# q transposed by the vector engine in 32x32 blocks, scores in 32x32 tensor-engine tiles: a fused attention and maxout kernel on one Trainium2 core

## The chip, the cores and the metric

The kernel runs on one core of a Trainium2 chip. The metric is the device time of one execution in microseconds (us). A profile shows a span from the first to the last instruction, which for this kernel is about 1.8 us shorter than the time. The granted clock is the TensorE clock that the profile records, as a share of full speed. A few executions fall into a much slower state (one of the kernel before at 287.87 us); these are left out of every comparison.

The engines: PE is TensorE (matmuls; PEld are its weight loads), DVE is VectorE, ACT is ScalarE, POOL is GpSimd (here it issues the input DMAs), SP is SyncE (the output DMAs). To evacuate a tile is to copy it from PSUM, where matmuls write, to SBUF. ffn is the part with w1, w2, w3 and w_out.

## The reference, cut to what matters

```python
# q, k, v: (8, 8, 576, 64); phi: (8, 8, 576, 32); float32
a    = softmax(phi, axis=2)                        # over the 576 tokens
k_m  = einsum('bhsm,bhsd->bhmd', a, k)             # 32 memory slots per head
v_m  = einsum('bhsm,bhsd->bhmd', a, v)
attn = softmax(q @ k_m^T / 8, axis=-1)             # 576 x 32 per head
x    = (attn @ v_m).transpose(0, 2, 1, 3).reshape(4608, 512)
h    = maximum(maximum(x @ w1, x @ w2), x @ w3)    # 512 -> 768
out  = h @ w_out                                   # 768 -> 512
```

The kernel folds v_m into w1, w2 and w3 for each batch, and works with w1 - w3 and w2 - w3, so that the maxout is a relu, a maximum, and w3 @ w_out added at the end.

One remark on correctness. With these inputs the scores are so small that every softmax over the 32 slots is nearly flat: computing the reference on a CPU with q set to zero changes the result by 8e-7 of its norm. So a comparison of results says next to nothing about whether the tokens of q are in the right order.

## The kernel before

A partition holds nine consecutive tokens of a head (`c` = 0..8), a pair of heads fills 128 partitions, and each of the 8 batches has four pairs (`j`). PE transposes q in 128x128 pieces into PSUM and DVE copies them to SBUF; columns then come in chunks, all tokens with the same `c` together.

```python
def att_q(b, jj):                      # jj = 0, 1: two pairs each; jj = 2: the ninth chunk
    ...
    pt = one_pool.tile([P, 2, NCP - 1, P], BF16, name="pt", tag="one")
    for i in range(2):
        for c in range(NCP - 1):
            nc.tensor.transpose(pt[:, i, c, :], qq[:, 2 * jj + i, 2 * c : 2 * c + 2, :], ident)
    nc.vector.tensor_copy(out=qT[:, 2 * jj : 2 * jj + 2, x : x + NCP - 1, :], in_=pt)
    ...

def att_score(b, g):                   # 64x32 tiles: 8 matmuls a step, two steps a batch
    ...
    nc.tensor.matmul(sc[M * j : M * (j + 1), par, 0 : nch * HP],
                     lhsT=km[par][r, g, j, :],
                     rhs=qT[r, j, c0 : c0 + nch, HP * g : HP * (g + 1)],
                     start=True, stop=True, tile_position=(HP * par, M * j))
    ...                                # exp on ACT, one call for each par
```

The order of all instructions is written by hand as a list of steps: Q transposes q, S the scores, M and R the softmax sums and reciprocals, X the multiply that gives attn, D the folds, F the twelve pieces of the first ffn layer, T the output tiles, E, B, N, K the phi exponentials, the k/v sums, their normalising and transposing. A plus sign means the next batch, two or three the ones after that, a minus sign the batch before. The steady loop is:

```python
run(b, "F0 F6 F1 F8 F4 F7 F2 F5 F10 F3 F9 T2- S0+ D1+ S1+ T3- Q0++ M0+ R0+")
run(b, "M1+ F11 Q1++ T0 R1+ T4- Q2++ E+++ D0+ X0+ B++ D3+ X1+ N++ D2+ T1 K++")
```

Output tiles are evacuated by DVE except one (`EVAC = {"D": "avaa", "T": "vvvav"}`, a for ACT, v for DVE), collected in pairs, and written by two DMAs a pair.

The softmax here doesn't subtract the row's maximum and nothing guards it: scores larger than these inputs give would overflow.

## Time and profile before

| | before |
|---|---|
| time, median of the fast runs | 186.08 us (185.88, 186.08, 186.31; a fourth run was slow) |
| span of the profiled run | 184.2 us |
| PE, DVE, ACT busy | 170.7, 110.1, 100.3 us |
| granted TensorE clock | 0.981 |
| last matmul to end of span | 6.3 us (177.9 to 184.2) |

The page gives each engine's busy time, then the span in 40 slices with a digit for the busy tenths, then the chain that ended last, followed back from the last instruction through whatever released each step. A microsecond saved off this chain is worth nothing until the chain moves. The lines themselves stand in the prediction.

### The profile page before, as it was taken

To read this page: it belongs to the slowest core of one execution; us is meant where nothing else is said; L and a number is where in the kernel's file an instruction comes from. 1 tells how busy PE (TensorE), PEld (TensorE's weight loads), DVE (VectorE), ACT (ScalarE), POOL (GpSimd) and SP (SyncE) were. 2 spreads that over 40 slices of the span, in tenths; PEclk is the share of its full clock that TensorE was granted. 3 is DMA by queue.
4 is the path that set the end of the run, shared out by engine and by line. 5 is a ranking of instruction groups with operands and counts; after the bars stand their busy time and mean duration, and the time that the engine had idled before them with its cause. 6 is when DMAs were issued, how large, how long until landed. Compare 5 with 4: busy or idle time off the path is not lost.

```text
span 184.2 us, 4510 instructions
## 1 busy us (share of the span) xinstructions
PE 170.7 (93%) x1940; PEld 97.8 (53%) x1940; DVE 110.1 (60%) x187; ACT 100.3 (54%) x158; POOL 28.3 (15%) x43
## 2 busy tenths in 40 slices
PE   7997997899999799999999999999999999999960
PEld 2454633554556557464756574657565744565420
DVE  5407338597396677757676677576766773564410
ACT  4100836846696776486637864866376646842010
POOL 7841121043212330005100400000000000000000
PEclk9999699999999999999999999999999999999996
DMA  5999999999999999998999699423021404240545
GB/s 155 162 208 208 209 210 273 208 276 206 272 255 222 308 228 253 255 216 261 287 253 188 112 197 249 120 62 92 25 57 62 114 4 116 57 114 4 136 94 168
DMA packets 21893, 31.75 MB, mean 172 GB/s; under 512 B 1265, under 2 KB 16369, under 8 KB 21873
## 3 DMA queue, kind: packets, MB, share of 16 engines
q0 software_dynamic: 16080, 21.43, 61.5%
q1 hardware_dynamic: 5792, 10.03, 19.6%
q8 instruction: 15, 0.25, 0.5%
q14 instruction: 6, 0.04, 0.1%
HBM read 39.32 MB, written 9.44 MB: 265 GB/s over the span
## 4 chain that ended last, share of the span: by engine, by line
PE 61%; DMA 23%; ACT 4%; POOL 4%; issue 3%; DVE 2%; POOLq 0%
PE po L412 22%; PE acc L385 22%; DMA w_sb<-in_moe_w_dram 12%; DMA qq<-in_q_dram 11%; PE po L421 6%; PE wps L360 3%; PE pt L262 2%; ACT wp L152 2%; POOL kvo L99 2%; PE sm L316 1%; PE po L430 1%; PE sc L292 1%; DVE w_sb L187 1%; POOL w_sb L113 1%; ACT r L335 1%
## 5 line engine op out<-in xcount | busy, mean ns | idle before, releaser
L385 PE MATMUL acc<-attn,wp 128*128 128x288 bf16 x384 | 52.5, 286 | 0.7 <-DVE wp L154 0.7
L412 PE MATMUL po<-wo_sb,hT 128*128 128x512 bf16 x216 | 52.6, 380 | 0.0
L397 DVE TENSOR_TENSOR hT<-acc,h 128x576 bf16<-128x576 f32 x48 | 35.5, 755 | 17.2 <-PE acc L385 16.0
L385 PEld LDWEIGHTS <-wp 128*128 128x128 bf16 x384 | 36.5, 98 | 13.2 <-DVE wp L154 1.0
L395 ACT ACTIVATE h<-acc 128x576 bf16<-128x576 f32 x48 | 29.7, 651 | 19.2 <-PE acc L385 19.2
L412 PEld LDWEIGHTS <-hT 128*128 128x128 bf16 x216 | 19.8, 98 | 23.9 <-issue 3.8
L154 DVE COPY ost<-po 128x512 f32<-128x512 f32 x24 | 16.6, 691 | 19.2 <-PE po L421 19.2
L152 ACT CAST wp<-wps 128x1024 bf16<-128x1024 f32 x24 | 23.4, 1014 | 7.9 <-PE wps L360 7.9
L302 ACT ACTIVATE e<-sc 128x320 bf16<-128x320 f32 (+1 forms) x32 | 10.7, 415 | 26.6 <-PE sc L292 26.6
L421 PE MATMUL po<-wp,attn 128*128 128x512 bf16 x64 | 19.0, 379 | 0.0
L265 DVE COPY qT<-pt 128x1024 bf16<-128x1024 bf16 x16 | 10.9, 686 | 6.8 <-PE pt L262 6.7
L143 PE MATMUL po<-warm 128*128 128x512 bf16 x44 | 12.6, 450 | 1.2 <-DVE warm L131 1.2
L152 ACT COPY ost<-po 128x512 f32<-128x512 f32 x8 | 4.7, 586 | 15.3 <-PE po L421 15.3
L107 POOL DMA_DIRECT2D qq<-in_q_dram x8 | 6.0, 744 | 43.1 <-PE pt L271 33.0
L329 ACT ACTIVATE ln<-sm 128x576 f32<-128x576 f32 x16 | 10.3, 645 | 2.2 <-PE sm L316 1.8
L340 DVE TENSOR_TENSOR attn<-e,r 128x576 bf16<-128x576 bf16 x16 | 11.4, 745 | 0.0
L360 PE MATMUL wps<-w_sb,vk 64*32 64x512 bf16 x96 | 9.3, 382 | 2.1 <-DVE w_sb L187 1.3
L335 ACT ACTIVATE r<-ln 128x576 f32<-128x576 f32 x16 | 10.9, 683 | 0.5
L204 ACT ACTIVATE e<-ph 128x1152 bf16<-128x1152 f32 (+1 forms) x9 | 9.5, 1051 | 2.2 <-DMA ph<-in_phi_dram 2.2
L262 PE MATMUL pt<-ident,qq 128*128 128x128 bf16 x128 | 9.6, 219 | 1.1 <-DMA qq<-in_q_dram 1.1
L421 PEld LDWEIGHTS <-attn 128*128 128x128 bf16 x64 | 6.3, 98 | 7.4
L262 PEld LDWEIGHTS <-qq 128*128 128x128 bf16 x128 | 8.2, 98 | 3.2 <-DMA qq<-in_q_dram 1.6
(51 smaller groups left out, 155.7 us busy)
## 6 DMA issues: line engine op xcount, KB each, us to landing
out_dram<-ost SPq DMA_DIRECT2D x32, 256.0 KB, 3.5
qq<-in_q_dram POOLq DMA_DIRECT2D x8, 576.0 KB, 17.6
ph<-in_phi_dram POOLq DMA_DIRECT2D x7, 576.0 KB, 18.6
kvo<-in_k_dram POOLq DMA_DIRECT2D x7, 576.0 KB, 17.5
kvo<-in_v_dram POOLq DMA_DIRECT2D x7, 576.0 KB, 19.5
w_sb<-in_moe_w_dram POOLq DMA_DIRECT2D x3, 768.0 KB, 19.0
out_dram<-ot SPq DMA_DIRECT2D x8, 128.0 KB, 2.4
wo_sb<-in_moe_w_out_dram POOLq DMA_DIRECT2D x1, 768.0 KB, 16.1
```

Source lines behind the costliest of these rows:

```text
L143: nc.tensor.matmul(po[:, 0:BANK], lhsT=warm[:, 0:P], rhs=warm, start=True, stop=True)
L152: nc.scalar.copy(out=out_, in_=in_)
L154: nc.vector.tensor_copy(out=out_, in_=in_)
L262: nc.tensor.transpose(pt[:, i, c, :], qq[:, 2 * jj + i, 2 * c : 2 * c + 2, :], ident)
L335: nc.scalar.activation(out=r, in_=ln, func=AF.Exp, scale=-1.0)
L340: nc.vector.tensor_tensor(out=attns[b // 2][:, g, (b % 2) * S : (b % 2 + 1) * S], in0=s["e2"][:, g, 0:S], in1=s["r", g], op=ALU.mult,)
L360: nc.tensor.matmul(ps[M * j : M * (j + 1), a, :], lhsT=s["vm"][a][r, a, j, :], rhs=w12[r, j, n * BANK : (n + 1) * BANK] if n < 3 else w3o[ ...
L385: nc.tensor.matmul(acc[:, h, 0:SH], lhsT=wps[b][:, g, w * DF + ft * P : w * DF + (ft + 1) * P], rhs=attn[:, g, c0 : c0 + SH], start=(g == ...
L395: nc.scalar.activation(out=h1, in_=a, func=AF.Relu)
L397: nc.vector.tensor_tensor(out=hT[:, ft, (b % 2) * S : (b % 2 + 1) * S].rearrange("p (h n) -> p h n", h=2), in0=a, in1=s["h1", ft], op=ALU.max,
L412: nc.tensor.matmul(po, lhsT=hT[:, fc, c0 : c0 + P], rhs=wo_sb[:, fc, :], start=(fc == 0), stop=False,)
L421: nc.tensor.matmul(po, lhsT=attn[:, g, c0 : c0 + P], rhs=wp3s[b][:, g, :], start=False, stop=(g == NG - 1),)
```

## The change

The intent: free PE of 160 transposes of q, by letting DVE transpose 32x32 blocks directly from SBUF to SBUF. The write of that transpose puts the tokens into their true order, so 128 columns are 128 consecutive output rows and each output tile is one plain DMA. As only 32 of the 64 head dimensions then share a block row, the scores become 32 matmuls a batch in sixteen 32x32 tiles, accumulated over two halves. Work is shared out anew between ACT and DVE, and the instruction order is new. The core of the diff:

```diff
-    EVAC = {"D": "avaa", "T": "vvvav"}
+    EVAC = {"D": "aass", "T": "aaava"}      # s: half on ACT, half on DVE
 ...
-    def att_q(b, jj):
+    def att_q(b, n):
 ...
+            s["qT"] = work.tile([P, NP, 2, SH], BF16, name="qT")
+        nc.vector.transpose(
+            out=s["qT"][:, :, n].rearrange("p j (r c) -> p j c r", c=NC),
+            in_=loaded[b]["q"].rearrange("p j c d -> p (j c) d")[:, :, R * n : R * (n + 1)],
+        )
 ...
+        for h in range(2):
+            for j in range(NP):
+                for a in range(NG):
+                    for t in range(2):
+                        r = slice(R * (2 * a + t), R * (2 * a + t + 1))
+                        nc.tensor.matmul(
+                            sc[a][M * j : M * (j + 1), t, 0:SH],
+                            lhsT=kvt[r, 1 + h, M * j : M * (j + 1)],
+                            rhs=qT[r, j, h, :],
+                            start=(h == 0),
+                            stop=(h == 1),
+                            tile_position=(R * (2 * a + t), M * j),
+                        )
 ...
+        ot = opool.tile([P, DM], FP32, name="ot")
+        evacuate("T", t, ot, po)
+        r0 = (b // 2) * 2 * S + c0
+        nc.sync.dma_start(out=out[r0 : r0 + P, :], in_=ot)
 ...
-        run(b, "F0 F6 F1 F8 F4 F7 F2 F5 F10 F3 F9 T2- S0+ D1+ S1+ T3- Q0++ M0+ R0+")
-        run(b, "M1+ F11 Q1++ T0 R1+ T4- Q2++ E+++ D0+ X0+ B++ D3+ X1+ N++ D2+ T1 K++")
+        run(b, "S+ B++ N++ D0+ T4- F0 F10 F1 F8 F11 F4 F2 F5 F6 E+++ F7 K++ F9 M0+ T3-")
+        run(b, "M1+ Q0++ F3 R0+ R1+ T2- D2+ D1+ D3+ X1+ Q1++ T1 T0 X0+")
```

`(r c) -> c r` means that the 32 elements of one block row are written nine elements apart: 2-byte elements at a step of 18 bytes.

More of the change, by code (lines that the diff above doesn't have):

```diff
@@ L37 @@
     NC = S // HP
-    NCP = (NC + 1) // 2
+    R = 32
     DM = H * D
@@ L41 @@
     FT = DF // P
-    EVEN = NCP * HP
     SH = S // 2
@@ L49 @@
     quad = ctx.enter_context(tc.tile_pool(name="quad", bufs=4))
+    opool = ctx.enter_context(tc.tile_pool(name="opool", bufs=6))
     acc_pool = ctx.enter_context(
@@ L145, in warm_up @@
             )
-    EVAC = {"D": "avaa", "T": "vvvav"}
+    EVAC = {"D": "aass", "T": "aaava"}
     def evacuate(kind, n, out_, in_):
-        if EVAC[kind][n] == "a":
+        e = EVAC[kind][n]
+        if e == "s":
+            nc.scalar.copy(out=out_[:, 0], in_=in_[:, 0])
+            nc.vector.tensor_copy(out=out_[:, 1], in_=in_[:, 1])
+        elif e == "a":
             nc.scalar.copy(out=out_, in_=in_)
@@ L228, in att_kv_norm @@
         nc.vector.reciprocal(out=rden, in_=kvp[:, :, 2 * D])
-        kvn = work.tile([P, NG, 2 * D], BF16, name="kvn")
+        kvn = work.tile([P, 3, P], BF16, name="kvn")
+        nc.vector.tensor_tensor(
+            out=kvn[:, 0].rearrange("p (a d) -> p a d", a=NG),
+            in0=kvp[:, :, D : 2 * D],
+            in1=rden.unsqueeze(2).to_broadcast([P, NG, D]),
+            op=ALU.mult,
+        )
         for g in range(NG):
+            kn = kvn[:, 1:3, HP * g : HP * (g + 1)]
             nc.vector.tensor_scalar_mul(
-                out=kvn[:, g], in0=kvp[:, g, 0 : 2 * D], scalar1=rden[:, g : g + 1]
+                out=kn.rearrange("p h (t d) -> p h t d", t=2),
+                in0=kvp[:, g, 0:D]
+                .rearrange("p (h d) -> p h d", h=2)
+                .unsqueeze(2)
+                .to_broadcast([P, 2, 2, R]),
+                scalar1=rden[:, g : g + 1],
             )
@@ L238, in att_kv_t @@
         s = st[b]
-        kvt = one_pool.tile([P, NG, NP, M], BF16, name="kvt", tag="one")
-        for g in range(NG):
-            nc.tensor.transpose(kvt[:, g], s["kvn"][:, g], ident)
-        kv = work.tile([P, NG, NP, M], BF16, name="kv")
-        nc.vector.tensor_copy(out=kv, in_=kvt)
-        vk = work.tile([P, NG, NP, M], BF16, name="vk")
-        for u in range(2):
-            nc.vector.tensor_copy(
-                out=vk[HP * u : HP * (u + 1)], in_=kvt[HP * (1 - u) : HP * (2 - u)]
-            )
@@ L249, in att_kv_t @@
-        s.update(km=(kv, vk), vm=(vk, kv))
-    def att_q(b, jj):
+        ps = one_pool.tile([P, 3, P], BF16, name="kvtp", tag="one")
+        for n in range(3):
+            nc.tensor.transpose(ps[:, n], s["kvn"][:, n], ident)
+        kvt = work.tile([P, 3, P], BF16, name="kvt")
+        nc.vector.tensor_copy(out=kvt, in_=ps)
+        s["kvt"] = kvt
+    def att_q(b, n):
         s = st.setdefault(b, {})
-        qq = loaded[b]["q"]
         if "qT" not in s:
-            s["qT"] = work.tile([P, NP, NCP, P], BF16, name="qT")
-        qT = s["qT"]
-        x = b % 2
-        if jj < NP // 2:
-            pt = one_pool.tile([P, 2, NCP - 1, P], BF16, name="pt", tag="one")
-            for i in range(2):
-                for c in range(NCP - 1):
-                    nc.tensor.transpose(
-                        pt[:, i, c, :], qq[:, 2 * jj + i, 2 * c : 2 * c + 2, :], ident
-                    )
-            nc.vector.tensor_copy(
-                out=qT[:, 2 * jj : 2 * jj + 2, x : x + NCP - 1, :], in_=pt
-            )
-        else:
-            pt = one_pool.tile([P, NP, P], BF16, name="pt", tag="one")
-            for j in range(NP):
-                nc.tensor.transpose(pt[0:HP, j, :], qq[:, j, NC - 1, :], ident)
-            nc.vector.tensor_copy(
-                out=qT[0:HP, :, 0 if x else NCP - 1, :], in_=pt[0:HP]
-            )
@@ L276 @@
-    attns = {}
-    def att_score(b, g):
-        s = st[b]
-        km, qT = s["km"], s["qT"]
-        x = b % 2
-        if "e2" not in s:
-            s["e2"] = work.tile([P, NG, S + HP], BF16, name="e2")
-            if x == 0:
-                attns[b // 2] = work.tile([P, NG, 2 * S], BF16, name="attn")
-        sc = acc_pool.tile([P, 2, BANK], FP32, name="sc", tag="acc")
-        for par in range(2):
-            nch = NCP - par
-            c0 = x * par
-            r = slice(HP * par, HP * (par + 1))
-            for j in range(NP):
-                nc.tensor.matmul(
-                    sc[M * j : M * (j + 1), par, 0 : nch * HP],
-                    lhsT=km[par][r, g, j, :],
-                    rhs=qT[r, j, c0 : c0 + nch, HP * g : HP * (g + 1)],
-                    start=True,
-                    stop=True,
-                    tile_position=(HP * par, M * j),
-                )
-        for par in range(2):
-            nch = NCP - par
+            s["qT"] = work.tile([P, NP, 2, SH], BF16, name="qT")
@@ new lines, in att_q, with att_score @@
+        nc.vector.transpose(
+            out=s["qT"][:, :, n].rearrange("p j (r c) -> p j c r", c=NC),
+            in_=loaded[b]["q"].rearrange("p j c d -> p (j c) d")[:, :, R * n : R * (n + 1)],
+        )
+    attns = {}
+    def att_score(b):
+        s = st[b]
+        kvt, qT = s["kvt"], s["qT"]
+        e2 = s["e2"] = work.tile([P, NG, S], BF16, name="e2")
+        if b % 2 == 0:
+            attns[b // 2] = work.tile([P, NG, 2 * S], BF16, name="attn")
+        sc = [
+            acc_pool.tile([P, 2, BANK], FP32, name="sc", tag="acc") for _ in range(NG)
+        ]
+        for h in range(2):
+            for j in range(NP):
+                for a in range(NG):
[8 more added lines that the diff above has]
+                            tile_position=(R * (2 * a + t), M * j),
+                        )
+        for a in range(NG):
@@ L302, in att_score @@
             nc.scalar.activation(
-                out=s["e2"][:, g].rearrange("p (c u n) -> p c u n", u=2, n=HP)[
-                    :, 0:nch, par, :
-                ],
-                in_=sc[:, par, 0 : nch * HP].rearrange("p (c n) -> p c n", n=HP),
+                out=e2[:, a].rearrange("p (t n) -> p t n", t=2),
+                in_=sc[a][:, :, 0:SH],
                 func=AF.Exp,
@@ L361, in fold @@
                     ps[M * j : M * (j + 1), a, :],
-                    lhsT=s["vm"][a][r, a, j, :],
+                    lhsT=s["kvt"][r, 0, M * j : M * (j + 1)],
                     rhs=w12[r, j, n * BANK : (n + 1) * BANK] if n < 3 else w3o[r, j, :],
@@ L437, in ffn2 @@
                     )
-        if t < 4:
-            if b not in osts:
-                osts[b] = work.tile([P, 4, DM], FP32, name="ost"), set()
-            ost, done = osts[b]
-            evacuate("T", t, ost[:, t], po)
-            done.add(t)
-            t0 = t - t % 2
-            if {t0, t0 + 1} <= done:
-                rows = out[b * S : (b + 1) * S, :].rearrange("(p c) d -> p c d", c=NC)
-                for u in range(2):
-                    c0 = 2 * t0 + (u + b) % 2
-                    nc.sync.dma_start(
-                        out=rows[:, c0 : c0 + 3 : 2, :],
-                        in_=ost[HP * u : HP * (u + 1), t0 : t0 + 2],
-                    )
-        else:
-            ot = work.tile([P, DM], FP32, name="ot")
-            evacuate("T", t, ot, po)
-            for u in range(2):
-                bb = b - 1 + u
-                rows = out[bb * S : (bb + 1) * S, :].rearrange("(p c) d -> p c d", c=NC)
-                nc.sync.dma_start(out=rows[:, NC - 1, :], in_=ot[HP * u : HP * (u + 1)])
+        ot = opool.tile([P, DM], FP32, name="ot")
+        evacuate("T", t, ot, po)
+        r0 = (b // 2) * 2 * S + c0
+        nc.sync.dma_start(out=out[r0 : r0 + P, :], in_=ot)
     issued = set()
-    loads = ((load_ph, "E"), (load_kv, "B"), (load_q, "Q0 Q1 Q2"))
+    loads = ((load_ph, "E"), (load_kv, "B"), (load_q, "Q0 Q1"))
     def issue(b, n):
@@ L475, in issue @@
             "Q": lambda: att_q(b, i),
-            "S": lambda: att_score(b, i),
+            "S": lambda: att_score(b),
             "M": lambda: att_sum(b, i),
@@ L500, in run @@
             issue(b + w.count("+") - w.count("-"), w.rstrip("+-"))
-    issue(0, "Z28")
+    issue(0, "Z24")
     att_exp(0, halves[0])
@@ L509 @@
     done(0, "B")
-    run(0, "N Z7 Q0 Q1 Q2 K S0 S1 W0 M0 R0 M1 R1")
+    run(0, "N Z9 K Q0 Q1 S W0 W1 M0 R0 W2 M1 R1 V0")
     for w in """
-        W1@0 W2@0 V0@0 O1@0 X1@0 X0@0 O2@0 O3@0 D0@0 V1@0 O0@0 V2@0 F2@0 D1@0
-        F0@0 D2@0 F10@0 F1@0 D3@0 F4@0 F3@0 E@1 F11@0 F8@0 F5@0 B@1 N@1 F9@0
-        K@1 F6@0 Q0@1 D3@1 Q2@1 F7@0 Q1@1 E@2 T1@0 S0@1 S1@1 D1@1 T0@0 M1@1
-        R1@1 T3@0 B@2 D0@1 M0@1 N@2 K@2 R0@1 Q0@2 D2@1 X0@1 D0@2 X1@1 E@3
-        D1@2 T2@0 F6@1 F0@1 Q1@2 F1@1 F10@1 F4@1 D3@2 F7@1 F2@1 Q2@2 F11@1 F5@1
-        F8@1 F3@1 S0@2 B@3 N@3 D2@2 S1@2 Q0@3 M0@2 Q2@3 R0@2 F9@1 Q1@3 M1@2
-        X0@2 T0@1 R1@2 X1@2 T1@1 K@3 E@4
+        O0@0 X0@0 O1@0 X1@0 O2@0 D0@0 O3@0 F0@0 V1@0 V2@0 F2@0 F4@0 F6@0 D1@0 D2@0
+        D3@0 F1@0 E@1 F7@0 F3@0 F5@0 F10@0 B@1 N@1 F8@0 F9@0 F11@0 K@1 T2@0 D3@1
+        Q0@1 D0@1 D2@1 Q1@1 T0@0 T3@0 E@2 S@1 B@2 M1@1 M0@1 N@2 R1@1 K@2 Q0@2 R0@1
+        Q1@2 T1@0 D1@1 X1@1 S@2 X0@1 D3@2 F6@1 F0@1 F7@1 F10@1 F8@1 F2@1 F1@1 F9@1
+        F4@1 F11@1 E@3 F3@1 F5@1 M1@2 B@3 R1@2 M0@2 Q0@3 E@4 N@3 R0@2 T1@1 K@3 D0@2
+        D2@2 Q1@3 X0@2 X1@2 D1@2 T0@1
     """.split():
@@ L522 @@
     for b in range(2, B - 1):
-        run(b, "F0 F6 F1 F8 F4 F7 F2 F5 F10 F3 F9 T2- S0+ D1+ S1+ T3- Q0++ M0+ R0+")
-        run(b, "M1+ F11 Q1++ T0 R1+ T4- Q2++ E+++ D0+ X0+ B++ D3+ X1+ N++ D2+ T1 K++")
-    run(B - 1, "F0 F2 F3 F8 F1 T2- F10 F9 F4 T4- F6 F5 F11 F7 T3- T2 T4 T1 T0 T3")
+        run(b, "S+ B++ N++ D0+ T4- F0 F10 F1 F8 F11 F4 F2 F5 F6 E+++ F7 K++ F9 M0+ T3-")
+        run(b, "M1+ Q0++ F3 R0+ R1+ T2- D2+ D1+ D3+ X1+ Q1++ T1 T0 X0+")
+    run(B - 1, "F8 F4 T4- F9 F5 F2 F0 T3- F10 F6 F3 F7 F11 F1 T2- T1 T3 T0 T4 T2")
 _INS = ['q', 'k', 'v', 'phi', 'moe_w1', 'moe_w2', 'moe_w3', 'moe_w_out']
```

## The prediction

> **What bounds the kernel now.** I read the page's table of busy time first, then the 40 slices, then the chain that ended last, then busy time by stretch, then the groups.
>
> ```profile
> PE 170.7 (93%) x1940; PEld 97.8 (53%) x1940; DVE 110.1 (60%) x187; ACT 100.3 (54%) x158; POOL 28.3 (15%) x43
> ...
> PE   7997997899999799999999999999999999999960
> ...
> DMA  5999999999999999998999699423021404240545
> ```
>
> TensorE is full from about slice 15 to the end, and the DMA engines are full up to about slice 23 (106 us). So the two compete to be the bound early on, and only TensorE is left later. The chain in order of time says where one hands over to the other:
>
> ```profile
> 7.92 21.91 DMA w_sb<-in_moe_w_dram
> ...
> 42.44 20.58 DMA qq<-in_q_dram
> 63.06 0.62 PE pt L262 x8
> ...
> 69.12 5.59 PE acc L385 x44
> ```
>
> The load of q for batch 3 was issued at 42.44 us and landed at 63.06 us, and the PE transposes that use it waited for it. It lay 20.6 us in the queue behind other loads: before 63 us the clock is the arrival of data. From 63 to 177.9 us nearly every piece of the chain is PE work. The steady loop, by stretch (start:end, length; then busy us of PE, PEld, DVE, ACT, POOL; clock; DMA share):
>
> ```profile
> 69.00:88.40 19.40, 19.22 (x241) 11.57 (x239) 12.87 (x23) 12.08 (x19) 3.05 (x5) 1.00 1.11 247
> 88.40:105.90 17.50, 17.32 (x228) 10.62 (x227) 12.05 (x22) 12.04 (x19) 2.23 (x3) 1.00 0.98 208
> 105.90:125.10 19.20, 19.02 (x238) 11.40 (x237) 12.71 (x23) 12.09 (x19) 0.00 (x0) 1.00 0.74 150
> 125.10:142.60 17.50, 17.32 (x229) 10.61 (x227) 12.05 (x22) 11.03 (x18) 0.00 (x0) 1.00 0.25 62
> ```
>
> One batch takes 18.4 us on average (19.3 with a fifth token tile, 17.5 without), PE is busy 99% of it, DVE and ACT about 66%. So here a microsecond of PE work removed is a microsecond of time, as long as ACT and DVE keep up.
>
> [...] No DVE transpose is in this trace, [...] 512 fp32 elements out of PSUM took 691 ns and 1024 took 1216 ns, so 1.03 ns an element and 166 ns fixed; 128 elements give 297 ns[...]. [...] The trace agrees that tiles run side by side (24 fold matmuls of 512 columns took 0.77 us in the chain, three rounds of 8); the 32x32 mode isn't in it.
>
> **The change, part by part.** The groups concerned:
>
> ```profile
> L262 PE MATMUL pt<-ident,qq 128*128 128x128 bf16 x128 | 9.6, 219 | 1.1 <-DMA qq<-in_q_dram 1.1
> L265 DVE COPY qT<-pt 128x1024 bf16<-128x1024 bf16 x16 | 10.9, 686 | 6.8 <-PE pt L262 6.7
> L154 DVE COPY ost<-po 128x512 f32<-128x512 f32 x24 | 16.6, 691 | 19.2 <-PE po L421 19.2
> L152 ACT COPY ost<-po 128x512 f32<-128x512 f32 x8 | 4.7, 586 | 15.3 <-PE po L421 15.3
> L272 DVE COPY qT<-pt 64x512 bf16<-64x512 bf16 x8 | 3.3, 408 | 0.1
> L246 DVE COPY vk<-kvt 64x256 bf16<-64x256 bf16 x16 | 4.6, 288 | 0.3
> ```
>
> PE loses 20 q transposes a batch. In the chain 8 of them take 0.45 us, 56 ns each, so 1.12 us a batch and 9.0 us in all. It gains one K/V transpose a batch (0.06 us). The scores go from 16 matmuls in 64x32 tiles, 0.14 us for a group of 8 in the chain, to 32 in 32x32 tiles of 288 columns. [...] the 72 small matmuls of L215 took 0.92 us, 12.8 ns each, so 32 take 0.41 us, 0.13 more than before. Net: about 0.94 us less PE a batch, 7.5 us in all.
>
> DVE, whole kernel: less 14.2 us (q evacuations), 6.9 (the kv and vk copies, 4.6 + 2.3) and 13.8 (20 of 28 output evacuations go to ACT, at 691 ns); plus 16 block transposes of 1152 elements, estimated by the line above at 1.35 us, 21.6 us; plus about 6 us for one wider kvt copy, a third normalising step and fold halves instead of one whole fold. 110 becomes about 103 us. It isn't the bound.
>
> ACT: 20 more output evacuations at 586 ns (+11.7), folds +1.3 (16 whole at 1014 and 16 halves at 586 ns for 24 whole), score exponentials 16 of 576 elements at some 650 ns instead of 32 small ones (-2.9). 100 becomes about 110 us. In the loop, per batch: relu 6 x 0.651 = 3.9, exp of phi 1.16, scores 1.3, ln and exp 2 x (0.645 + 0.683) = 2.7, folds 2.0 + 1.2, outputs 3.5 x 0.586 = 2.05: 14.3 us of about 17.4, 82%. This is the new tightest neighbour of PE.
>
> Output DMAs: 40 become 36, each 128 whole consecutive rows, the same bytes and the same 2 KB rows. This can matter only at the end. Now the last matmul is at 177.87 us, the evacuation ends at 178.48, two DMAs of 256 KB are issued after it (0.6 us each), and the span ends at 184.2. With one DMA of 256 KB after the last evacuation, one issue and some of the sharing go: I take 0.9 us.
>
> What of the 7.5 us counts? Batches 4 to 7 have their q work inside the PE-bound loop: 4 x 0.94 = 3.8 us gained. Batches 0 to 2 have it before 63 us, where data arrive no sooner: weights and batches 0 to 3 come through the same queue in the same order, so PE only comes earlier to a wait. Batch 3 is the doubtful one. In the new order the DVE[...] stands at the transposes of q of batch 3 until about 63 us; then it has 1.35 us of transpose and about 1.1 of normalising before PE can transpose K/V (about 65.7), and the second transpose, two multiplies and ACT's delayed work (exp of phi 4, ln/exp, three folds, two outputs: some 7 us from about 65) follow. By this I get the scores of batch 3 on PE at about 69.5. The next matmuls are the K/V sums of batch 4, now at the head of the loop instead of near its end, whose loads were issued at 49.5 and 50.2 and, at the median queue time of 17.5 and 19.5 us, land at 67 to 70. The ffn of batch 2 would begin at 73 to 74 us, with 3.4 us of work done (scores, sums, a fold, a tile) that the old loop still had ahead at 69.1. That is between nothing and 1 us behind the old kernel. Against this, loads may run slightly ahead of my estimate, and the old kernel has small waits there too. I take zero for the passage.
>
> Sum: -3.8 (loop) - 0.9 (tail) + 0 (passage) = -4.7; span 184.2 becomes 179.5, and with the 1.85 us between span and measured time (186.03 against 184.2) the time is 181.3 us, 2.6% faster.
>
> **Rivals.** (a) All of it counts: if the loads don't hold the new order up, batch 3 and part of the earlier ones count too, up to 7.5 + 0.9 us, 177.7 us. For it: PE is 86 to 98% busy even before 63 us. Against it: the 20.6 us queue wait in the chain, and slices of 9 for DMA. (b) ACT takes PE's place: at 82% of the loop, with three PSUM accumulator buffers shared by scores, sums, folds and ffn, each ffn tile waits for a relu when several even tiles come together. 0.3 to 0.6 us a batch would eat half of the gain: about 183.5 us. For it: score exponentials, a whole fold and an output all lie on ACT just ahead of the first ffn tiles. Against it: the slack is 3 us a batch and the order was chosen anew with this split. (c) The block transpose is much slower[...] since it writes 2-byte elements 18 bytes apart. At twice my estimate DVE has 14.8 us a batch, and waits of PE on it would bring about 185 us. [...] (d) 32x32 tiles don't overlap fully[...]: 0.2 to 0.4 us a batch, 2 us in all.
>
> **Range and chances.** The centre is 181.3; (a) pulls to 178, (b) and (d) to 184. I take 178.2 to 184.3 for 8 in 10. 2% faster is 182.4, one microsecond above the centre: 0.64 for faster, 0.31 for within 2%, 0.05 for slower.
>
> **What would show it.** The loop should take about 17.4 us a batch, PE still 98% busy, no pt transposes of q, and 16 DVE transposes near 1.35 us with DVE near 103 and ACT near 110 us. The chain should still have a DMA piece (q or k/v) ending between 60 and 71 us, with more PE waiting there than before. The time from last matmul to end should fall from 6.3 to about 5.4 us. It is wrong if ACT pieces make up many per cent of the chain in the loop (b), if transposes last over 2 us (c), if the scores take over 0.6 us a batch (d), or if there is no DMA wait after 40 us (a).

What came from outside this case's traces and runs is cut, here and in the expectations below, and the cuts are marked. The sum is -3.8 - 0.9 + 0 = -4.7 us, on a span of 184.2. Three of the figures behind it are estimates for something that the trace of the kernel before doesn't hold. The 1.35 us of a block transpose takes over the rate of DVE's copies out of PSUM (691 ns for 512 elements, 1216 for 1024). The 0.41 us of the scores takes over the 12.8 ns of each of the 72 small matmuls. The 0.9 us of the tail is 0.6 us for an issue, as measured, and a guess for the rest. The sizes given to rivals (b), (c) and (d) are guesses as well.

## The result, and the profile after

The changed kernel takes 243.27 us in the median (242.33 to 243.59, four fast runs), against 186.08 before. The ratio is 1.306, with a 95% interval of 1.301 to 1.312. Here and below a ratio is the mean time of one kernel's fast runs over that of the other's of the same rounds, so not quite the ratio of the medians. The predicted 181.3 us (178.2 to 184.3) was far off.

The busy times and two slice rows of the changed kernel's page:

```profile
PE 177.3 (74%) x1894; PEld 94.5 (39%) x1914; DVE 162.6 (67%) x159; ACT 111.3 (46%) x170; POOL 28.3 (12%) x43
...
PE   8940797960905957399498949895869497999992
...
PEclk9996599997685797989869986999799979999999
```

PE is no longer full: its row has holes up to slice 34. DVE has 162.6 us instead of the predicted 103, ACT 111.3 as predicted (110). And the clock row, all nines before but for slice 5 and the end, has dips. The costliest group says where DVE's time is:

```profile
L270 DVE STREAM_TRANSPOSE qT<-qq 128x1152 bf16<-128x1152 bf16 x16 | 83.4, 5260 | 0.0
```

Sixteen transposes at 5.26 us each, where 1.35 had been estimated: 62 us more than planned, and DVE is 60 us over the plan. The rest of DVE's account was right. Two loops of the steady state in the view by stretch (start:end, length; busy us of PE, PEld, DVE, ACT, POOL; clock; DMA share; GB/s):

```profile
113.90:138.00 24.10, 19.25 (x222) 10.35 (x223) 19.10 (x19) 13.15 (x21) 2.22 (x3) 0.86 0.63 135
138.00:163.60 25.60, 20.65 (x231) 10.97 (x233) 19.03 (x19) 13.77 (x22) 0.74 (x1) 0.87 0.34 83
```

A batch takes 24 to 26 us. No engine is full: DVE, the busiest beside PE, has 19 us. What fills the batch is a chain that goes back and forth between engines, as the chain in order of time (start us, us, what) shows for one loop:

```profile
113.88 5.17 DVE qT L270
119.05 0.59 DVE hT L394
...
119.68 0.67 PE wps L357 x7
...
120.38 0.59 ACT wp L153
...
120.99 0.69 DVE wp L154
121.69 0.66 DVE attn L337
122.35 5.18 DVE qT L270
...
127.57 0.45 PE sc L292 x16
128.02 1.18 ACT e L301 x2
```

DVE took the instructions of this loop in the order in which they are written (Q0, F3, the folds, X1, Q1, X0). The first transpose keeps a maximum of the ffn, a fold and a multiply waiting behind it: the last matmul for that maximum (hT, F3) had ended at 113.88 us, and the maximum began at 119.05, when the transpose was through. The second comes just ahead of the scores of the next batch, and PE's next ffn needs the end of that chain. All transposes together are 34.1% of the chain, 82 us of 241.2.

The dips in the clock cost more on top. After one of the longest stalls the chain has:

```profile
64.54 10.22 DVE qT L270 x2
...
76.06 7.57 PE acc L382 x40
```

Forty ffn matmuls took 7.57 us here, 189 ns apart; the kernel before did 44 in 5.59 us, 127 ns apart. PE had waited 3.5 and 4.7 us for the two transposes (the idle time before L292), and in pieces of 1 us the granted clock is 1.00 from 64 to 70 us, 0.88 from 70 to 71, 0.50 from 71 to 81 us, and 1.00 again from 81 us to the next gap. Some 21 of the matmuls fall into the first 4.94 us, about 235 ns apart, and 22 into the 2.64 us after 81, about 120 ns apart. In two other gaps (52.3 to 60.6 us, with one short group of matmuls in it, and 116.2 to 119.7 us) the clock also falls to 0.50 while PE stands, at about 57.1 and 118.6 us, and comes back when PE has been at work again for 3 to 6 us. The mean clock of the whole span is 0.887, against 0.981. So the trace shows the order of things, first the gap and then the slow clock; no run made such gaps without the slow transposes, and what makes the clock fall is not shown.

### The profile page after: what moved, and what is told of

It is laid out like the page before. It is cut to its first block, busy times and chain, and to the rows that moved or that the text cites. A ratio compares the mean times of both kernels' runs of the same rounds, so it can differ in the third digit from the quotient of the medians.

```text
span 241.2 us, 4434 instructions
## 1 busy us (share of the span) xinstructions
PE 177.3 (74%) x1894; PEld 94.5 (39%) x1914; DVE 162.6 (67%) x159; ACT 111.3 (46%) x170; POOL 28.3 (12%) x43
## 4 chain that ended last, share of the span: by engine, by line
PE 44%; DVE 41%; ACT 7%; DMA 3%; issue 2%; POOL 1%; ACTq 0%; POOLq 0%
DVE qT L270 34%; PE acc L382 20%; PE po L410 9%; DMA kvo<-in_v_dram 3%; DVE wp L154 3%; PE po L419 2%; PE po L175 2%; PE kvp L219 2%; ACT wp L153 2%; PE wps L357 2%; DVE attn L337 2%; PE sm L313 2%; PE sc L292 1%; DVE hT L394 1%; ACT e L301 1%
## 5 line engine op out<-in xcount | busy, mean ns | idle before, releaser
L270 DVE STREAM_TRANSPOSE qT<-qq 128x1152 bf16<-128x1152 bf16 x16 | 83.4, 5260 | 0.0
L410 PE MATMUL po<-wo_sb,hT 128*128 128x512 bf16 x199 | 57.6, 423 | 1.9 <-issue 1.4
L156 ACT COPY ot<-po 128x512 f32<-128x512 f32 x28 | 16.4, 586 | 39.6 <-PE po L419 34.8
L292 PE MATMUL sc<-qT,kvt 32*32 32x288 bf16 x256 | 6.0, 322 | 35.8 <-DVE qT L270 35.8
L301 ACT ACTIVATE e<-sc 128x576 bf16<-128x576 f32 x16 | 9.5, 648 | 47.3 <-PE sc L292 47.3
L154 DVE CAST wp<-wps 128x512 bf16<-128x512 f32 x16 | 11.1, 697 | 15.1 <-ACT wp L153 15.1
L292 PEld LDWEIGHTS <-kvt 32*32 32x32 bf16 x256 | 2.4, 89 | 40.5 <-issue 36.7
L156 ACT CAST wp<-wps 128x1024 bf16<-128x1024 f32 x16 | 16.4, 1023 | 4.0 <-PE wps L357 4.0
L357 PE MATMUL wps<-w3o,kvt 64*32 64x512 bf16 x64 | 3.9, 466 | 14.2 <-DVE hT L394 14.1
L153 ACT CAST wp<-wps 128x512 bf16<-128x512 f32 x16 | 9.4, 600 | 10.5 <-PE wps L357 10.5
L337 DVE TENSOR_TENSOR attn<-e,r 128x576 bf16<-128x576 bf16 x16 | 12.8, 822 | 0.0
L158 DVE COPY ot<-po 128x512 f32<-128x512 f32 x8 | 5.7, 718 | 9.7 <-PE po L419 9.7
```

The lines of the kernel that those rows point to most:

```text
L153: nc.scalar.copy(out=out_[:, 0], in_=in_[:, 0])
L154: nc.vector.tensor_copy(out=out_[:, 1], in_=in_[:, 1])
L156: nc.scalar.copy(out=out_, in_=in_)
L270: nc.vector.transpose(out=s["qT"][:, :, n].rearrange("p j (r c) -> p j c r", c=NC), in_=loaded[b]["q"].rearrange("p j c d -> p (j c) d")[: ...
L301: nc.scalar.activation(out=e2[:, a].rearrange("p (t n) -> p t n", t=2), in_=sc[a][:, :, 0:SH], func=AF.Exp, scale=0.125,)
L337: nc.vector.tensor_tensor(out=attns[b // 2][:, g, (b % 2) * S : (b % 2 + 1) * S], in0=s["e2"][:, g, 0:S], in1=s["r", g], op=ALU.mult,)
```

## The experiments

| run | write of qT | order | time, median | against before |
|---|---|---|---|---|
| the change | scattered | new | 243.27 | 1.306 |
| e2_dense_only | dense (tokens permuted) | new | 185.88 | 0.997 |
| e3_dense_exp | dense, exp reorders | new | 185.84 | 0.998 |
| e4_dense_pe | dense, PE reorders | new | 188.19 | 1.011 |
| e7_q1_early | dense, exp reorders | new, one step moved | 182.32 | 0.980 |
| e8_q1_early_whole_folds | dense, exp reorders | as e7, folds whole | 183.13 | 0.982 |
| e5_old_order | dense, exp reorders | old | 180.70 | 0.969 |
| e6_old_order_t1_act | dense, exp reorders | old, one tile to ACT | 181.99 | 0.977 |
| e11_late_q | dense, exp reorders | old, q steps of batches 2 and 3 later | 180.09 | 0.966 |
| e9_old_order_scattered | scattered | old | 237.10 | 1.274 |

e1_forms and e10_more_steps measure single instructions, in one run each, whose state is unknown; they are told first. The "old order" is the order of steps of the kernel before together with its split of evacuations between ACT and DVE (`EVAC`): no run changes the one without the other, except e6 and e8 (the split alone) and e7 (one step alone).

### e1_forms: the disputed instruction by itself

```diff
+    # after the last tile of the kernel before; src = 36 runs of 64 bytes, ps_ = 36 dense runs
+    nc.vector.transpose(out=d.rearrange("p (j r c) -> p j c r", j=4, c=9), in_=src)   # L531
+    nc.vector.transpose(out=d.rearrange("p (k r) -> p k r", r=32), in_=src)           # L532
+    nc.vector.transpose(out=d.rearrange("p (k r) -> p k r", r=32), in_=ps_)           # L533
+    nc.vector.transpose(out=d.rearrange("p (j r c) -> p j c r", j=4, c=9), in_=ps_)   # L534
+    # L535, L536: dense input, output steps of 2 and 4 elements; L537, L538: 128 elements, step 1 and 9
+    nc.vector.tensor_copy(out=d.rearrange("p (j r c) -> p j c r", j=4, c=9), in_=...) # L539
+    nc.vector.tensor_copy(out=d, in_=...)                                             # L540
```

> The kernel before, with ten DVE instructions appended after its last tile, each on a line of its own, that measure the disputed cost alone (the outputs stay right). Theory A, the scattered write: a transpose of 1152 elements with the output step of 9 elements (18 bytes), as in the change, takes about 5.2 us whether its input is dense or in runs of 64 bytes; with a dense output it takes 1.3 to 1.4 us; with steps of 2 and 4 elements also about 5 us[...] or between the two if the cost grows with the step. Theory B, the input in runs of 64 bytes: the form with a dense input and the scattered output takes 1.4 us and the one with a dense output but the input of the change takes 5.2 us. Theory C, the transpose itself[...]: all forms of 1152 elements take about 5.2 us, and 128 elements take about 0.7 us[...]. A plain copy with the same scattered output tells whether scatter costs every DVE operation (over 4 us) or the transpose alone (about 1.3 us).

The timeline of DVE (start us, us):

```profile
182.72 1.38 DVE L532 STREAM_TRANSPOSE w_sb<-kvo 128x1152 bf16<-128x1152 bf16 x1
184.13 1.38 DVE L533 STREAM_TRANSPOSE w_sb<-kvo 128x1152 bf16<-128x1152 bf16 x1
185.54 5.21 DVE L534 STREAM_TRANSPOSE w_sb<-kvo 128x1152 bf16<-128x1152 bf16 x1
190.78 1.46 DVE L535 STREAM_TRANSPOSE w_sb<-kvo 128x1152 bf16<-128x1152 bf16 x1
192.27 2.73 DVE L536 STREAM_TRANSPOSE w_sb<-kvo 128x1152 bf16<-128x1152 bf16 x1
195.03 0.31 DVE L537 STREAM_TRANSPOSE w_sb<-kvo 128x128 bf16<-128x128 bf16 x1
...
196.15 2.69 DVE L539 COPY w_sb<-kvo 128x1152 bf16<-128x1152 bf16 x1
198.87 0.46 DVE L540 COPY w_sb<-kvo 128x1152 bf16<-128x1152 bf16 x1
```

With a dense output the transpose takes 1.38 us, whether its input is dense (L533) or in runs of 64 bytes (L532). With the scattered output it takes 5.21 us even from a dense input, and 5.22 from the input of the change (L531). So theory A holds, B and C fall. The dense 128-element form takes 311 ns, where the prediction's line gave 297; with an output step of 9 elements (L538) it takes 736. The cost grows with the step: 1.46 us at 2 elements, 2.73 at 4, 5.21 at 9. A plain copy with the same scatter takes 2.69 us instead of 0.46: the copy pays for the scatter too, 2.2 us against 3.8 for the transpose.

### e10_more_steps: how the cost depends on the step

```diff
+    # after the kernel before: transposes of n elements, blocks apart, output step s
+    nc.vector.transpose(out=pd[:, 0:n*s].rearrange("p (k r s) -> p k r s", r=32, s=s)[:, :, :, 0], in_=...)
+    # n = 1024: s = 2, 3, 4, 6, 8, 9;  n = 288: s = 9, 16, 32;  copies, n = 1024: s = 2, 4, 8, 9
```

> The kernel before with thirteen DVE instructions appended: transposes of 1024 elements (32 blocks) with an output step of 2, 3, 4, 6, 8 and 9 elements, of 288 elements with steps of 9, 16 and 32, and plain copies of 1024 elements with steps 2, 4, 8 and 9. If the cost grows with the step and then levels off: about 1.3 us at step 2, 2.4 at 4, 4.5 to 4.7 at 8 and 9, and the 288-element forms alike at 9, 16 and 32 (about 1.4 us). If it keeps growing with the step, 8 is dearer than 4 in proportion and the 32 form costs over three times the 9 form. If it is the odd step[...] that costs, 3 and 9 are dear and 4, 6 and 8 are not. In the first run the blocks of the change interleave (block c writes one element beside block c-1); here they lie apart, so if interleaving is the cost, step 9 takes about 1.3 us here.

| step (elements) | 2 | 3 | 4 | 6 | 8 | 9 |
|---|---|---|---|---|---|---|
| transpose of 1024, ns | 1305 | 1876 | 2442 | 3577 | 4703 | 4641 |
| copy of 1024, ns | 740 | | 1301 | | 2430 | 2424 |

With 288 elements, steps of 9, 16 and 32 take 1433, 1381 and 1427 ns. So the cost rises evenly with the step (0.55 ns an element for each further 2 bytes of step) up to 8 elements, 16 bytes, and is flat in the steps measured beyond (4641 ns at 9 against 4703 at 8, and the three of 288 elements). Odd steps are not special (1876 ns at 3, halfway between 1305 and 2442), and interleaved blocks are not needed for it.

At a step of 4 elements, 8 bytes, the transpose already takes 1.9 times as long as at 2 (2442 and 1305 ns), and the copy 1.8 times (1301 and 740). What in the write costs this, and why it levels off at 16 bytes, no run shows.

### e2_dense_only: the write of the transposes alone

```diff
-            out=s["qT"][:, :, n].rearrange("p j (r c) -> p j c r", c=NC),
+            out=s["qT"][:, :, n].rearrange("p j (c r) -> p j c r", c=NC),
```

> The changed kernel with one edit: the transposes write qT dense, in the order in which the blocks come, with no other engine touched. The tokens come out permuted, so the result is wrong on purpose. Theory A (scattered write): each transpose about 1.35 us, DVE busy about 100 us, the time falls from 243 to about 181 us (178 to 184), the granted clock back to about 0.98. Theory C (the transpose itself is slow) or B (its input): nothing changes, 5.2 us each and 243 us. Rival D (the new order of instructions, the split of ACT work or the 32x32 tiles cost much besides): transposes are fast but the time stays over 186 us.

The tokens of a batch now come out permuted, wrong; as told above, the comparison doesn't notice. The time is 185.88 us, ratio 0.997 (0.994 to 1.000). This one edit gives back 57 of the 57 us lost. Two lines of its page:

```profile
PE 162.9 (88%) x1914; PEld 90.1 (49%) x1914; DVE 102.3 (56%) x159; ACT 110.6 (60%) x170; POOL 28.3 (15%) x43
...
L270 DVE STREAM_TRANSPOSE qT<-qq 128x1152 bf16<-128x1152 bf16 x16 | 21.7, 1365 | 0.9 <-DMA qq<-in_q_dram 0.9
```

The transposes take 1365 ns, DVE 102.3 us (predicted 103), ACT 110.6 (110), the clock is 0.986. But it is not the predicted 181: rival D holds in part, some 4.6 us are still missing. The chain at the joint, where one batch ends and the next begins, shows where a part of them is:

```profile
102.36 0.59 ACT ot L156
...
103.32 1.03 ACT wp L156
104.35 0.50 ACT wp L153
...
104.87 0.69 DVE wp L154
105.56 0.67 DVE attn L337
106.23 1.30 DVE qT L270
...
107.57 0.34 PE sc L292 x16
107.91 0.86 PE kvp L219 x72
```

For 5.2 us the chain is not on PE: an output tile, a whole fold and half a fold on ACT, the other half on DVE, the multiply, the second transpose; only then can the scores run. In the four steady loops PE stands idle for 2.9 us (71.77 us long, 68.88 busy); in those of the kernel before it is 0.7 (73.52 and 72.81). Note also that the DVE half starts when the ACT half ends (104.85 and 104.87): the profile puts 17.4 us of waiting of the DVE halves down to the ACT halves, so here splitting a fold into halves did not make the halves run together.

### e3_dense_exp and e4_dense_pe: two ways to put the tokens back in order

```diff
 # e3: the exponential reads PSUM with a step of 32 elements and writes densely
-                out=e2[:, a].rearrange("p (t n) -> p t n", t=2),
-                in_=sc[a][:, :, 0:SH],
+                out=e2[:, a].rearrange("p (t r c) -> p t r c", t=2, c=NC),
+                in_=sc[a][:, :, 0:SH].rearrange("p t (c r) -> p t r c", c=NC),
 # e4: the score matmul reads qT with a step of 32 elements
-                            rhs=qT[r, j, h, :],
+                            rhs=qT[r, j, h, :].rearrange("p (c r) -> p r c", c=NC),
```

> The same dense transposes, and the score exponentials on ACT put the tokens back in order by reading PSUM with a step of 32 elements; the result is right. Theory A: as with the dense write alone, about 181 us, if ACT reads PSUM with a step at the same rate (0.65 us for 576 elements); if the stepped read costs ACT as the stepped write cost DVE, its exponentials take about 2.4 us instead of 0.65 and the time rises by several us.

> The same dense transposes, and the score matmuls on PE put the tokens back in order by reading qT with an inner step of 32 elements (64 bytes); the result is right. Theory A: about 181 us[...]; if[...] the 32 matmuls of a batch take about 1 us instead of 0.4 and the time is 184 to 186 us.

e3: 185.84 us in the median of its three fast runs, ratio 0.998 (0.994 to 1.002), the same as e2. The reordering on ACT is free: in e5, a fast run with the same edit, an exponential of 576 elements takes 648 ns at a step of 128 bytes, and 648 without it in e2. e4: 188.19 us, ratio 1.011 (1.006 to 1.015). The score matmuls there:

```profile
L292 PE MATMUL sc<-qT,kvt 32*32 32x288 bf16 x256 | 12.2, 687 | 4.8 <-DVE qT L270 4.8
```

One takes 687 ns instead of 291 in e2, and all together are busy 12.2 us instead of 5.8. PE's read pays for stepping 64 bytes as well, 2.4 times here. e3 lies 4.8 us above the expected 181 us, as e2 does, and e4 2.2 to 4.2 above the 184 to 186 guessed for a slow read: that is what e2 left open, and e5 traces it to the order.

### e5_old_order: the parts of the change in the order of the kernel before

```diff
-    EVAC = {"D": "aass", "T": "aaava"}
+    EVAC = {"D": "avaa", "T": "vvvav"}
 # steps as in the kernel before, without Q2 and S1; the loop is
+        run(b, "F0 F6 F1 F8 F4 F7 F2 F5 F10 F3 F9 T2- S+ D1+ T3- Q0++ M0+ R0+")
+        run(b, "M1+ F11 Q1++ T0 R1+ T4- E+++ D0+ X0+ B++ D3+ X1+ N++ D2+ T1 K++")
```

> Dense transposes and tokens put back in order by the exponential, as in the run with the right result, but with the instruction order and the split of evacuations of the kernel before (the separate q evacuation and second score step left out); the 32x32 scores, the token tiles and the output DMAs stay as changed. The question is where the 4.7 us of the prediction went once the transposes are fast (185.9 instead of 181.3). Theory P, the new order: its loop takes 18.1 us a batch because ACT fold halves, DVE fold halves, a multiply, the transpose, scores and exponentials stand one behind the other at the joint of two batches, and batch 3 waits there too. Then the old order gives about 17.4 us a batch and 180 to 182.5 us in all. Theory Q, the parts themselves (32x32 scores[...], DVE transposes between other DVE work) cost what the q transposes cost: then about 186 us here too.

180.70 us (179.96 to 181.05, six runs), ratio 0.969 (0.966 to 0.972). Theory P holds, Q falls: 32x32 scores and DVE transposes give what was expected of them, and the new order had lost it. The busy times of this page, then the same stretch as the first of the prediction's loop lines:

```profile
PE 162.1 (91%) x1916; PEld 88.0 (49%) x1916; DVE 114.5 (64%) x171; ACT 98.8 (55%) x142; POOL 28.3 (16%) x43
```

```profile
69.00:88.40 19.40, 19.23 (x244) 11.07 (x243) 14.01 (x22) 12.67 (x19) 2.98 (x4) 1.00 1.16 266
```

In this stretch PE is as full as in the kernel before, with 8.6 us less to do in all. That does not hold for the next loop (87.06 to 104.50 us): there PE is busy 16.32 of 17.44 us, against 17.34 of 17.52 before, and the chain lies on ACT for 5 us (an output tile, both ln and exp, the exponential of phi, a fold). This loop gains 0.08 us, the three others 0.74 to 1.03: in one loop of four, ACT does take PE's place, as rival (b) of the prediction has it. From one ffn start to that four batches later the chain goes from 68.56 to 139.34 us, 17.70 us a batch. The kernel before has 69.12 to 142.64, 18.38.

### e6_old_order_t1_act: one more output tile on ACT

```diff
-    EVAC = {"D": "avaa", "T": "vvvav"}
+    EVAC = {"D": "avaa", "T": "vavav"}
```

> The same with output tile 1 also evacuated on ACT, so that DVE carries about 109 and ACT about 103 us instead of 114 and 98. Theory P with DVE tight: 0.5 to 1.5 us less than the run beside it; if neither engine is near the path, no difference above 0.3%.

A miss in the other direction: 181.99 us, ratio 0.977 (0.974 to 0.979), 1.3 us slower than e5. The totals were as planned (DVE 109.6, ACT 102.9), but in this run DVE waited 5.1 us for ACT's relus before its maxima, where in e5 it was at most 1.2. So balanced totals did not help here. That the relus behind the added tile are what cost the 1.3 us fits this wait, but no run tests it.

### e7_q1_early and e8_q1_early_whole_folds: mending the new order

```diff
 # e7
-        run(b, "M1+ Q0++ F3 R0+ R1+ T2- D2+ D1+ D3+ X1+ Q1++ T1 T0 X0+")
+        run(b, "M1+ Q0++ F3 R0+ R1+ Q1++ T2- D2+ D1+ D3+ X1+ T1 T0 X0+")
 # e8, besides
-    EVAC = {"D": "aass", "T": "aaava"}
+    EVAC = {"D": "avav", "T": "aaava"}
```

> Dense transposes, right result, the changed order with one move: in the loop the second q transpose of a batch goes ahead of output tile 2 and the folds, where DVE is idle. Theory P: the 1.3 us of transpose leave the joint in four loops, so the time falls by up to 4 x 0.8 to 1.3 us, to about 182 us. If the joint is set by the folds on ACT alone, the gain is under 1 us. Theory Q: no change, 186 us.

> As the run before it, with folds evacuated whole, 0 and 2 on ACT and 1 and 3 on DVE, instead of two whole on ACT and two in halves, of which the DVE half waits for the ACT half. Theory P: another 0.5 to 1 us a batch at the joint, 179 to 181 us in all, with the waits of DVE folds on ACT folds gone (17.4 us in the dense run). Theory Q: no change, 186 us.

e7: 182.32 us, ratio 0.980 (0.977 to 0.983). Moving one DVE instruction of 1.37 us in the loop gains 3.5 us against e3 (185.84), some 0.9 us for each of the four loops that have it. In its chain the stretch from the folds to the scores is now PE work throughout; what is left at the joint, in two of the four loops, is an output tile and the score exponentials on ACT, 1.7 us. The four loops (74.33 to 142.68 us) take 68.35 us, PE is busy for 68.08 of them. So the transpose at the end of the joint cost 3.5 of the 5.1 us between e3 and e5. What e7 still lacks against e5 lies before the loops: its ffn of batch 2 begins at 74.33 us, 5.8 us later than that of e5 at 68.56, though only 3.4 us of PE's other work come before it in exchange.

e8: two of its six runs counted as slow; the four fast ones have a median of 183.13 us and give 0.982 (0.975 to 0.988). The waits of DVE folds on ACT folds are gone by construction, and nothing was gained beyond e7. The expected further 0.5 to 1 us a batch did not come; once the transpose had left the joint, the copies of the folds were no longer on the chain of the loops, in e7 as in e8. Whether whole folds cost something of their own isn't settled by an interval this wide.

### e9_old_order_scattered: the fourth corner

```diff
 # e5 with the write and the exponential of the change
-            out=s["qT"][:, :, n].rearrange("p j (c r) -> p j c r", c=NC),
+            out=s["qT"][:, :, n].rearrange("p j (r c) -> p j c r", c=NC),
```

> The old order and the old split of evacuations with the scattered write of the change (tokens in order from the transpose, exponential not stepped); the result is right. This is the fourth corner: write dense or scattered, order new or old. DVE busy should be about 114.5 + 16 x 3.85 = 176 us. Theory A alone (the slow write is the whole loss): the scattered write costs about as much in either order, some 50 to 60 us, so 230 to 240 us here. If the new order is what makes the slow transposes so dear (they stand at its joint), the old order loses much less, under 30 us, about 205 to 210 us.

237.10 us, ratio 1.274 (1.270 to 1.277), DVE 174.3 us busy, clock 0.864. The write costs 56.4 us in the old order (237.1 - 180.7) and 57.4 in the new (243.3 - 185.8). The order costs 5.1 us with the dense write and 6.2 with the scattered one. So the two causes add up, to within 1.1 us, and the scattered write is ten times the larger.

### e11_late_q: waiting for q less

```diff
 # e5 with four steps of the first batches moved
-        ... R0@1 Q0@2 D2@1 X0@1 D0@2 X1@1 ... F0@1 Q1@2 F1@1 F10@1 F4@1 ...
+        ... R0@1 D2@1 X0@1 D0@2 X1@1 ... F0@1 Q0@2 F1@1 F10@1 Q1@2 F4@1 ...
-        ... D2@2 Q0@3 M0@2 R0@2 F9@1 Q1@3 M1@2 X0@2 T0@1 R1@2 X1@2 T1@1 ...
+        ... D2@2 M0@2 R0@2 F9@1 M1@2 X0@2 T0@1 R1@2 X1@2 Q0@3 Q1@3 T1@1 ...
```

> The run with the old order and dense transposes, with the q transposes of batches 2 and 3 moved behind the attention multiplies of the batch before, so that the in-order DVE doesn't hold those multiplies back while q is still in the DMA queue (in the chain of that run q of batch 2 landed at 51.2 us and the ffn of batch 1 began at 55). If that wait sets the later time: 1 to 4 us less than its 180.7. If the arrival of k, v and q of batch 3 holds it again at about 62 us, no change beyond 0.5 us.

That DVE kept the written order is seen in the change, where a maximum waited 5.2 us behind a transpose (113.88 to 119.05 us). In e5 q landed at 51.16 us; the transpose then ran from 51.18 and the two multiplies from 52.56.

180.09 us (179.71 to 180.84, six runs), ratio 0.966 (0.964 to 0.969). The interval overlaps with that of e5 (0.966 to 0.972), from other rounds, so a gain over e5 isn't shown: the medians differ by 0.6 us, and of the expected 1 to 4 us at most 1.6 fits into the two intervals. Its chain has a new wait in place of the old:

```profile
37.20 16.88 DMA ph<-in_phi_dram
```

phi of batch 3 lands at 54.08 us; the exponential on ACT waits for it, and the relu written behind that starts at 55.17. Early on it is the flow of data that counts, as the prediction said, and with one wait moved another transfer was next.

## Why the prediction was wrong

**The step that failed** is the cost of the block transpose: "plus 16 block transposes of 1152 elements, estimated by the line above at 1.35 us". The estimate was right for a dense write (1.38 us in e1, 1365 ns in e2). The instruction in the diff doesn't write densely, and takes 5.26 us. The rate was taken from DVE copies that write densely (691 ns for 512 elements, 1216 for 1024), and the access pattern of the output was not part of the estimate. The term of the sum that was mis-sized is thus 21.6 us of DVE, measured as 83.4; and with it fell "It isn't the bound": DVE makes up 41% of the chain, PE 44%.

**Rival (c)** named this mechanism with the right reason and was given the wrong size and too little weight. It took twice the estimate and 185 us; it is 3.9 times, and 243 us. "At twice my estimate DVE has 14.8 us a batch" led to thinking in shares of a batch. What counted was that DVE, with its later work in line behind, is taken up for 5.2 us, twice a batch, in a chain that PE waits for.

**The passage and the loop** (0 and -3.8) are the second error, hidden under the first, and e2 lays it open. With fast transposes in the new order the four loops from 74.75 to 146.52 us gain 1.75 us on those of before (71.77 against 73.52), not 3.8; and 0.9 of it is only a k/v sum that the new order has done before its first loop (216 of these matmuls in the stretch instead of 288). The size of the loop term was right all the same: in e7, with one transpose moved, the four loops take 68.35 us, with that sum added about 69.3, so 17.3 us a batch, where 17.4 was predicted. What was wrong is that the new order would let PE run so. The passage: e2 begins the ffn of batch 2 at 74.75, after the 3.4 us of work that the old loop still had ahead at 69.12. So it is 2.2 us behind, where zero was taken. The estimate had said 73 to 74 and "between nothing and 1 us behind". Its mechanism came only in part: the DVE was to stand at q of batch 3 until its data came at about 63 us, but in e2 that transpose, at 62.79, waits for no data. It is ACT that waits, 1.4 us, for phi of batch 4, which lands at 64.88 us; its delayed work, and DVE and the scores behind that, follow as described. The whole span of e2, in differences to the kernel before: ffn of batch 2 later by 5.6, loops -1.75, from the ffn of batch 6 to the last matmul -1.8 (33.4 against 35.2, some 2.5 us of that work being done already), tail -2.1, sum -0.1 us. Rival (b), ACT in PE's place, came in another form than foreseen: the chain of e2 shows few waits for relus, but folds, a multiply and a transpose behind one another at the joint.

**What was right.** PE's saving: with fast transposes PE is busy 162 to 163 us, 8 us less than before (7.5 predicted). DVE and ACT totals, to 1 us, in e2 (by some luck: the score exponentials were to save ACT 2.9 us and saved 1.2, from 10.7 to 9.5, as the sum of mean times had counted overlaps twice). The 32x32 tiles: 32 matmuls appear in the chain of e5 with 0.39 us (0.41 predicted), so (d) falls. The tail: from the last matmul to the end it is 4.2 us (174.7 to 178.9 in e5, 237.0 to 241.2 in the change), 2.1 less than before, where 0.9 was taken. The total of 181.3 us agrees with the 180.7 of e5, but by luck, not by the same terms: loops -2.7 (four times 18.38 - 17.70), tail -2.1, and -0.5 for the rest, mostly the passage (68.56 against 69.12), sum -5.3 us of span (184.2 to 178.9).

**What stays open.** How much of the 57 us is stall and how much the lower clock was not separated: no run kept PE busy with dummy work during the transposes. An estimate from the busy times: PE is busy 177.3 us in the change and 162.9 in e2 for the same matmuls (20 of their records are missing from the first), so the slower clock accounts for some 15 us at most, and the rest is waiting. How the 5 us of "order" divide between the order of steps and the split of evacuations is known only so far as e7 goes, which moves one step and gets 3.5 back. Why the cost climbs with the step from 2 elements on, and levels off at 8, is not explained. In e8 nothing is settled about whole folds.

## What to carry to other kernels

Before moving a layout change to another engine, price the write pattern and not only the number of elements: a dense write with the reordering left to the reader that did it for free (here ACT reading PSUM, 648 ns both ways) turned 243 us into 186. Then judge the instruction order apart from the parts: the same parts in the old, proven order, with the old split of evacuations, gave 180.7. And on an engine that takes its instructions in the written order, as DVE did here, put an instruction where nothing urgent stands behind it; 1.4 us moved by a few places was worth 3.5 us.
